# A fused attention and expert layer: other durations in the scheduler's table, and one more dependency for the weight conversions

## The chip, the cores and the metric

The program runs on one core of a Trainium2 chip. The metric is the device time of one execution in microseconds; for the kernel before it is 677.38 us, the median of three runs (677.03 to 679.04). The engines of the core have a queue each and work through it in order: TensorE (PE, with its weight loads as PEld), VectorE (DVE), ScalarE (ACT), GpSimd (POOL), and SyncE (SP), which here issues all transfers.

## The reference

The inputs are q, k, v of shape (4 batches, 12 heads, 448 positions, 64) and two weight matrices, 768 x 2048 and 2048 x 768, all float32.

```python
scores = scale * np.matmul(q, k.transpose(0, 1, 3, 2))
scores = np.where(mask, -1000000000.0, scores)          # causal
scores = scores - np.max(scores, axis=-1, keepdims=True)
attn = np.exp(scores)
attn = attn / (np.sum(attn, axis=-1, keepdims=True) + 1e-09)
x = np.matmul(attn, v)          # then (batch, head) x (seq, dim) -> 1792 tokens x 768
h = x @ w_in
g = h * np.clip(h + 3.0, 0.0, 6.0) / 6.0
out = g @ w_out
```

## The kernel before

Positions are cut into four tiles of C = 112. The first tile of all four batches (448 columns) is group 0; the remaining R = 336 positions of each batch are groups 1 to 4. For each group the attention of six head pairs gives x, and then the two dense layers run on it (`group`, L602): 16 chunks of w_in (768 columns each) make h, the gate gives g, and 24 chunks of w_out (512 columns) make the output.

For precision every operand of a dense layer is split into a rounded high part and the remainder: xh and xl, gh and gl, wh and wl, and for the scores op and kl. A product is three matmuls (`triple`, L596: L598, L599, L600), so a chunk of w_in takes 18 and a chunk of w_out 12. The high part is a cast by ScalarE or GpSimd (`move`: L238, L245), the remainder a subtraction by GpSimd or VectorE (`minus`: L250).

The weights come in as 64-bit words. In group 0 each chunk is turned into float32 bits on VectorE by three operations for each half chunk (L571, L573, L576; a w_out chunk has one such set), stored to `kept_w` for the later groups, cast and subtracted. The scratch of the conversion is a bank of tag "s".

The attention of group 0 (`first_pair`, L297) handles 112 rows of four batches at once: scores (L322, L329), row maxima (L336, L342), exponentials (L348, L360), sums (L363), `inverse` (L369, L370), normalisation on GpSimd (L377), transposes (L386), copies, and the product with v (L399). The attention of the others (`pair`, L410): scores (L453 in the first batch; L450 and L451 later), mask and row maximum in one VectorE operation (L476), exponential with its sum (L483), `inverse` (L492, L493), six normalisations per pair on GpSimd (L505, `scaled`), 18 transposes on PE in six turns (L516), copies, the product with v (L535). After the first dense layer of a chunk come ReLU (L621), the gate (L627), and the split into gh and gl. The accumulator has two banks ("mo"); L627 is the last to read one.

The order of the work is not written out by hand. A planner (`Flow`, L72) runs when the program is built: each operation has a key (its due time), its reads and writes, and the engines that can do it with a cost factor and a lag, as `{"P": 2, "D": (1, 1.0)}`: on GpSimd the base duration times 2, on VectorE times 1 but only from 1.0 us after it is ready. A free engine of the plan takes the ready operation with the lowest key whose buffers are free. What comes out is one fixed order for each engine; on the chip each engine follows its order and waits by semaphores. The base durations that matter here (n columns):

```python
def elem(n, psum=False):                 # minus, conversions
    return (n + 150) / 960
one(key, ways or {"A": 1}, (n + 200) / 1200, emit, r, w)     # move
```

Of the kernel before, what the change touches and what calls it, by code (L numbers as in the profile page):

```python
# [190 lines left out]
def tile_causal_attention_hardswish_moe(ctx: ExitStack, tc: tile.TileContext, q, k, v, w_in, w_out, out):  # L191
# [85 lines left out]
    def x_split(key, g, p, av, n):  # L277
        xh, xl = buf("xh", [128, S], F32R), buf("xl", [128, S], F32R)
        x_t[g, p] = xh, xl
        move(key, n, lambda: ap(xh)[:, :n], lambda: ap(av)[:, :n], [(av, 0)], [(xh, 0)], {"A": 1, "D": (1, .5)})  # L280
        y = av
        if g < 2:
            y = buf("r", [128, S])
            move(key, n, lambda: ap(y)[:, :n], lambda: ap(av)[:, :n], [(av, 0)], [(y, 0)], {"A": 1})
        minus(
            key + .01, n, lambda: ap(xl)[:, :n], lambda: ap(y)[:, :n], lambda: f(ap(xh)[:, :n]),
            [(y, 0), (xh, 0)], [(xl, 0)], {"P": 2, "D": (1, 1.0)} if g < 2 else {"D": 1},
        )
# [8 lines left out]
    def first_pair(p):  # L297
# [75 lines left out]
        one(t + 3.5, {"D": 1}, .5, inverse, [], sums)  # L373
# [36 lines left out]
    def pair(n):  # L410
# [15 lines left out]
        if b:  # L426
            for e in range(2):
                x, y, z = qk[e], op[e], kl[e]
                move(
                    t - 5, R + S, lambda x=x, y=y: ap(y), lambda x=x: ap(x), raw[4 * e:4 * e + 4] + [("step", t - 12)], [(y, 0), (y, 1)],  # L430
                    {"P": 1.1, "A": (1, .5)},
                )
                minus(
                    t - 4.9, S, lambda z=z: ap(z), lambda x=x: ap(x)[:, R:], lambda y=y: f(ap(y)[:, R:]),
                    [(x, 0, R), (x, 1, R), (y, 1)], [(z, 0)], {"D": 1, "P": (2, 1.0)},
                )
                minus(
                    t - 4.8, R, lambda y=y: ap(y)[64:, :R], lambda x=x: ap(x)[64:, :R], lambda y=y: f(ap(y)[64:, :R]),
                    [(x, 1, 0)], [(y, 0)], {"D": 1, "P": (2, 1.0)},
                )  # L440
# [57 lines left out]
        for e in range(2):  # L498
            for i in reversed(TILES):
                def scaled(g, e=e, i=i):  # L500
                    x, r = ap(pr[e, i]), ap(st)[:, e, 4 + i:5 + i]
                    if g == "A":
                        nc.scalar.activation(x, x, ACTF.Copy, scale=r)
# [3 lines left out]
                    t + 4.5 + .1 * e, {"P": 1}, (C * (i + 1) + 300) / 1100, scaled,  # L507
# [39 lines left out]
    def weights(g, i, t, early):  # L547
# [6 lines left out]
        else:  # L554
# [25 lines left out]
            for o in range(0, n, m):  # L580
# [6 lines left out]
                flow.op(t - T_W + .01, {"D": (1, 0)}, one_by_one, [(wd, 0)])  # L587
# [14 lines left out]
    def group(g):  # L602
# [3 lines left out]
        for i in range(NF):  # L606
# [19 lines left out]
            def gate(_, r=r, acc=acc):  # L626
# [9 lines left out]
                [(r, 0), (gh, i)], [(gl, i)], {"D": 1, "P": (1.9, .7)} if g else {"P": 2, "D": (1, 1.5)},  # L636
# [73 lines left out]
```

## Time and profile before

| | us |
|---|---|
| median of the runs | 677.38 |
| profiled execution | 677.73 |
| its span | 676.0 |
| busy PE / VectorE / ScalarE / GpSimd | 648.2 / 476.4 / 358.5 / 308.0 |

The span runs from the first to the last instruction. Busy time of an engine is the union of its instructions; for PE the ends of matmuls are modelled. A wait is put down to the engine that released it last. Durations of single instructions hold any time in which they were slowed, not only their bare work. Two numbers in a shape are partitions x elements. PEclk, the clock granted to PE, is given as a share of its upper level.

### The profile page before, as it was taken

To read this page: it belongs to the slowest core of one execution; us is meant where nothing else is said; L and a number is where in the kernel's file an instruction comes from. 1 tells how busy PE (TensorE), PEld (TensorE's weight loads), DVE (VectorE), ACT (ScalarE), POOL (GpSimd) and SP (SyncE) were. 2 spreads that over 40 slices of the span, in tenths; PEclk is the share of its full clock that TensorE was granted. 3 is DMA by queue.
4 is the path that set the end of the run, shared out by engine and by line. 5 is a ranking of instruction groups with operands and counts; after the bars stand their busy time and mean duration, and the time that the engine had idled before them with its cause. 6 is when DMAs were issued, how large, how long until landed. Compare 5 with 4: busy or idle time off the path is not lost.

```text
span 676.0 us, 12212 instructions
## 1 busy us (share of the span) xinstructions
PE 648.2 (96%) x4236; PEld 588.5 (87%) x4236; DVE 476.4 (70%) x945; ACT 358.5 (53%) x851; POOL 308.0 (46%) x346
## 2 busy tenths in 40 slices
PE   7789999999999989999999989999999999999998
PEld 5559878878788979999999879999889899999997
DVE  5999989986597877755688785666879743466432
ACT  3676565544446556555565555556545554444432
POOL 1558687655476266423356464442476502022000
PEclk9989999999999999999999999999999999999999
DMA  9998977796686544356844346556542334743452
GB/s 236 258 303 242 286 245 234 230 310 232 177 292 181 167 147 137 119 163 181 245 143 125 98 135 186 176 163 194 158 148 64 98 107 132 216 141 110 140 166 68
DMA packets 66877, 120.88 MB, mean 179 GB/s; under 512 B 16896, under 2 KB 33408, under 8 KB 66816
## 3 DMA queue, kind: packets, MB, share of 16 engines
q1 hardware_dynamic: 66816, 120.11, 59.1%
q8 instruction: 33, 0.54, 0.3%
q14 instruction: 28, 0.23, 0.1%
HBM read 101.99 MB, written 18.09 MB: 178 GB/s over the span
## 4 chain that ended last, share of the span: by engine, by line
PE 73%; POOL 10%; DVE 8%; issue 5%; ACT 2%; DMA 1%; SPq 1%; POOLq 0%; DVEq 0%; ACTq 0%
PE mo L598 19%; PE mo L600 18%; PE mo L599 18%; POOL pr L505 7%; PE s L535 6%; PE s L516 5%; PE s L450 2%; PE s L453 2%; PE s L451 2%; DVE wl L250 2%; DMA gh<-in_k_dram 1%; POOL gh L245 1%; SPq L229 1%; DVE r L627 1%; PE s L399 1%
## 5 line engine op out<-in xcount | busy, mean ns | idle before, releaser
L250 DVE TENSOR_TENSOR wl<-wd,wh 128x512 fp32r<-128x512 f32 (+1 forms) x155 | 141.3, 912 | 101.8 <-ACT wh L238 99.8
L238 ACT CAST wh<-wd 128x512 fp32r<-128x512 f32 (+1 forms) x160 | 112.8, 705 | 133.0 <-PE mo L599 100.4
L598 PE MATMUL mo<-xh,wh 128*128 128x336 f32 (+1 forms) x480 | 161.3, 336 | 2.7 <-DVE r L627 2.4
L598 PE MATMUL mo<-gh,wh 128*128 128x336 f32 (+1 forms) x480 | 160.3, 334 | 0.0
L600 PE MATMUL mo<-gh,wl 128*128 128x336 f32 (+1 forms) x480 | 156.5, 326 | 0.7 <-POOL wl L250 0.7
L599 PE MATMUL mo<-gl,wh 128*128 128x336 f32 (+1 forms) x480 | 156.5, 326 | 0.0
L600 PE MATMUL mo<-xh,wl 128*128 128x336 f32 (+1 forms) x480 | 156.3, 326 | 0.0
L599 PE MATMUL mo<-xl,wh 128*128 128x336 f32 (+1 forms) x480 | 155.5, 324 | 0.0
L505 POOL TENSOR_SCALAR pr<-pr,prow 112x224 f32<-112x224 f32 x144 | 105.5, 749 | 48.3 <-DVE prow L493 45.6
L598 PEld LDWEIGHTS mo<-xh,wh 128*128 128x128 f32 x480 | 90.5, 188 | 8.3 <-DVE r L627 5.2
L483 ACT ACTIVATE pr<-s,prow 112x448 f32<-112x448 f32 (+1 forms) x144 | 76.8, 540 | 36.4 <-DVE prow L476 36.3
L598 PEld LDWEIGHTS mo<-gh,wh 128*128 128x128 f32 x480 | 90.2, 188 | 4.2 <-issue 1.0
L600 PEld LDWEIGHTS mo<-gh,wl 128*128 128x128 f32 x480 | 90.2, 188 | 2.7 <-POOL wl L250 1.1
L599 PEld LDWEIGHTS mo<-xl,wh 128*128 128x128 f32 x480 | 91.0, 190 | 1.1
L599 PEld LDWEIGHTS mo<-gl,wh 128*128 128x128 f32 x480 | 90.3, 188 | 1.2
L600 PEld LDWEIGHTS mo<-xh,wl 128*128 128x128 f32 x480 | 90.2, 188 | 1.2
L476 DVE CUSTOM_DVE_ANT_0 s<-s,mask 112x448 f32<-112x448 f32 (+1 forms) x144 | 69.9, 532 | 25.0 <-PE s L451 19.9
L245 POOL TENSOR_SCALAR gh<-r 128x336 fp32r<-128x336 f32 x49 | 24.2, 494 | 116.4 <-DVE r L627 109.6
L250 POOL TENSOR_TENSOR wl<-op,wh 128x512 fp32r<-128x512 f32 (+1 forms) x38 | 56.9, 1498 | 37.6 <-ACT wh L238 35.3
L245 POOL TENSOR_SCALAR op<-qk 128x784 fp32r<-128x784 f32 x34 | 33.6, 993 | 74.9 <-PE s L451 64.0
L238 ACT COPY pt<-s 112x336 f32<-112x336 f32 x126 | 49.1, 443 | 25.9 <-PE s L516 25.6
L516 PE MATMUL s<-ident,pr 112*112 112x112 f32 x432 | 55.2, 261 | 7.0 <-POOL pr L505 6.6
(70 smaller groups left out, 868.6 us busy)
## 6 DMA issues: line engine op xcount, KB each, us to landing
wd<-kept_w SPq DMA_DIRECT2D x64, 384.0 KB, 3.8
wd<-kept_w SPq DMA_DIRECT2D x96, 256.0 KB, 2.7
wd<-in_w_in_dram SPq DMA_DIRECT2D x16, 768.0 KB, 6.3
wd<-in_w_out_dram SPq DMA_DIRECT2D x24, 512.0 KB, 5.2
qk<-in_k_dram SPq DMA_DIRECT2D x84, 112.0 KB, 2.9
qk<-in_q_dram SPq DMA_DIRECT2D x84, 84.0 KB, 2.8
kept_w<-op SPq DMA_DIRECT2D x16, 384.0 KB, 5.6
kept_w<-op SPq DMA_DIRECT2D x24, 256.0 KB, 5.6
```

What stands on the lines that cost most here:

```text
L238: nc.scalar.copy(o(), i()) if scale is None else nc.scalar.mul(o(), i(), scale)
L245: nc.gpsimd.tensor_scalar(o(), i(), 1.0, 1.0, ALU.mult, ALU.mult)
L250: (nc.gpsimd if e == "P" else nc.vector).tensor_tensor(o(), a(), b(), ALU.subtract)
L450: nc.tensor.matmul(dst, ap(op[e])[:, c], ap(op[e])[:, R:R + w], start=True, stop=False)
L476: lambda _, e=e, i=i, w=w, dst=dst: nc.vector.tensor_tensor_reduce(dst(), dst(), mask[:, S - w:], -0.125, 3.0e38, ALU.add, ALU.min, ap(st) ...
L483: lambda _, e=e, i=i, dst=dst: nc.scalar.activation(ap(pr[e, i]), dst(), ACTF.Exp, bias=ap(st)[:, e, i:i + 1], scale=-1.0, accum_out=ap(st ...
L505: nc.gpsimd.tensor_scalar(x, x, r, 1.0, ALU.mult, ALU.mult)
L516: nc.tensor.transpose(ap(tp)[:C, C * o:C * o + C], ap(pr[e, i])[:, C * j:C * j + C], ident)
L535: nc.tensor.matmul(ap(av)[64 * e:64 * e + 64, R - w:R], ap(vr)[:, j, e, :], ap(ph)[:, o:o + w], start=(j == 0), stop=(j == NC_ - 1),)
L598: nc.tensor.matmul(ps, ap(wh)[:, a], xh, start=start, stop=False)
L599: nc.tensor.matmul(ps, ap(wh)[:, a], xl, start=False, stop=False)
L600: nc.tensor.matmul(ps, ap(wl)[:, a], xh, start=False, stop=stop)
```

## The change

The cost factors of several subtractions and casts in the planner's table become larger, mostly those of GpSimd; the duration of a normalisation gets another formula. The reciprocal of each first pair (`inverse` in `first_pair`) also writes a token ("sums", p), and the conversion of every chunk but the first reads the token of the last pair, so that it is planned, and on the chip waits, behind that reciprocal. The rewritten call in `scaled` stands in a branch for ScalarE that no normalisation takes.

```diff
@@ -284,7 +284,7 @@
             move(key, n, lambda: ap(y)[:, :n], lambda: ap(av)[:, :n], [(av, 0)], [(y, 0)], {"A": 1})
         minus(
             key + .01, n, lambda: ap(xl)[:, :n], lambda: ap(y)[:, :n], lambda: f(ap(xh)[:, :n]),
-            [(y, 0), (xh, 0)], [(xl, 0)], {"P": 2, "D": (1, 1.0)} if g < 2 else {"D": 1},
+            [(y, 0), (xh, 0)], [(xl, 0)], {"P": 2.4, "D": (1, 1.0)} if g < 2 else {"D": 1},
         )
 
 
@@ -370,7 +370,7 @@
             nc.vector.reciprocal(r, r)
 
         sums = [(st, 0, 4)] + [(st, 1, 4 + b) for b in range(B)]
-        one(t + 3.5, {"D": 1}, .5, inverse, [], sums)
+        one(t + 3.5, {"D": 1}, .5, inverse, [], sums + [("sums", p)])
         for e in (1, 0):
             one(
                 t + 4, {"P": 1}, 1.05,
@@ -428,15 +428,15 @@
                 x, y, z = qk[e], op[e], kl[e]
                 move(
                     t - 5, R + S, lambda x=x, y=y: ap(y), lambda x=x: ap(x), raw[4 * e:4 * e + 4] + [("step", t - 12)], [(y, 0), (y, 1)],
-                    {"P": 1.1, "A": (1, .5)},
+                    {"P": 1.3, "A": (1, .5)},
                 )
                 minus(
                     t - 4.9, S, lambda z=z: ap(z), lambda x=x: ap(x)[:, R:], lambda y=y: f(ap(y)[:, R:]),
-                    [(x, 0, R), (x, 1, R), (y, 1)], [(z, 0)], {"D": 1, "P": (2, 1.0)},
+                    [(x, 0, R), (x, 1, R), (y, 1)], [(z, 0)], {"D": 1.25, "P": (2.2, 1.5)},
                 )
                 minus(
                     t - 4.8, R, lambda y=y: ap(y)[64:, :R], lambda x=x: ap(x)[64:, :R], lambda y=y: f(ap(y)[64:, :R]),
-                    [(x, 1, 0)], [(y, 0)], {"D": 1, "P": (2, 1.0)},
+                    [(x, 1, 0)], [(y, 0)], {"D": 1.3, "P": (2.6, 1.5)},
                 )
         st = buf("prow", [C, 2, 8])
         ps = {(e, i): bank("s") for i in TILES for e in range(2)}
@@ -500,11 +500,11 @@
                 def scaled(g, e=e, i=i):
                     x, r = ap(pr[e, i]), ap(st)[:, e, 4 + i:5 + i]
                     if g == "A":
-                        nc.scalar.activation(x, x, ACTF.Copy, scale=r)
+                        nc.scalar.mul(x, x, r)
                     else:
                         nc.gpsimd.tensor_scalar(x, x, r, 1.0, ALU.mult, ALU.mult)
                 one(
-                    t + 4.5 + .1 * e, {"P": 1}, (C * (i + 1) + 300) / 1100, scaled,
+                    t + 4.5 + .1 * e, {"P": 1}, min(.95, .2 + C * (i + 1) / 500), scaled,
                     [(st, e, 4 + i)], [(pr[e, i], 0)],
                 )
             for a, js in enumerate(((0,), (1,), (2, 3))):
@@ -584,7 +584,7 @@
                     (elem(m), lambda _, cv=cv, o=o, a=a: bits(cv, o, m, a), [[(cv, 0)], [(cv, 0)], [(wf, o)]][a])
                     for a in range(3)
                 ]
-                flow.op(t - T_W + .01, {"D": (1, 0)}, one_by_one, [(wd, 0)])
+                flow.op(t - T_W + .01, {"D": (1, 0)}, one_by_one, [(wd, 0)] + ([("sums", NPAIR - 1)] if i else []))
             dma(t - T_W, 512 * n, lambda: kept[i, :, :n], w, wk, [("kept", i)])
         move(t - T_W + .1, n, lambda: ap(wh)[:, :n], w, wk, [(wh, 0)], {"A": 1})
         minus(
@@ -633,7 +633,7 @@
             )
             minus(
                 t, n, lambda i=i: ap(gl)[:, i, :n], lambda r=r: ap(r)[:, :n], lambda i=i: f(ap(gh)[:, i, :n]),
-                [(r, 0), (gh, i)], [(gl, i)], {"D": 1, "P": (1.9, .7)} if g else {"P": 2, "D": (1, 1.5)},
+                [(r, 0), (gh, i)], [(gl, i)], {"D": 1.4, "P": (2.6, 1.0)} if g else {"P": 2.3, "D": (1.4, 1.5)},
             )
         for m in range(NK):
             acc, ob = bank("mo"), buf("r", [128, S])
```

## Rows read from the trace of the kernel before

**Rows 1.** The page, section 1: engine, busy us (share of the span) x instructions.

```profile
PE 648.2 (96%) x4236; PEld 588.5 (87%) x4236; DVE 476.4 (70%) x945; ACT 358.5 (53%) x851; POOL 308.0 (46%) x346
```

**Rows 2.** Windows: us, then busy of each engine (x instructions), clock, DMA share, GB/s.

```profile
24.00:49.00 25.00, 17.10 (x149) 11.07 (x145) 24.20 (x51) 18.20 (x56) 13.55 (x12) 0.86 0.91 270
49.00:160.00 111.00, 110.75 (x622) 93.81 (x622) 95.85 (x199) 62.27 (x144) 76.61 (x76) 1.00 0.83 267
160.00:212.00 52.00, 48.80 (x287) 41.60 (x284) 40.40 (x85) 25.67 (x66) 28.29 (x30) 1.00 0.69 209
212.00:560.00 348.00, 339.62 (x2317) 315.55 (x2317) 248.55 (x497) 196.24 (x471) 169.30 (x194) 1.00 0.50 148
```

**Rows 3.** Waits: engine, line <- awaited: us in total, times, longest.

```profile
PEld s L516 <- POOL pr L505: 10.0, 15, 1.5
...
PE s L516 <- POOL pr L505: 6.6, 12, 1.3
...
PEld mo L598 <- DVE r L627: 5.2, 9, 1.3
...
PE mo L598 <- DVE r L627: 2.4, 3, 1.1
```

**Rows 4.** Timeline of PE, 36 to 53 us: start, length, instruction [idle before].

```profile
45.64 0.99 PE L399 MATMUL s<-pt,gl 112*64 112x112 f32 x16 [0.73 <-ACT pt L238]
46.56 2.42 PE L453 MATMUL s<-qk 64*112 64x448 f32 x8
48.91 0.48 PE L598 MATMUL mo<-xh,wh 128*128 128x448 f32 x1
...
52.62 0.36 PE L598 MATMUL mo<-xh,wh 128*128 128x448 f32 x1
```

**Rows 5.** Timeline of VectorE, 35 to 42 us.

```profile
35.74 0.55 DVE L571 TENSOR_SCALAR s<-wd 128x384 int32<-128x384 int32 x1
...
40.71 0.61 DVE L363 TENSOR_REDUCE prow<-pr 112x4 f32<-112x448 f32 x1
...
41.56 0.20 DVE L370 RECIPROCAL prow<-prow 112x8 f32<-112x8 f32 x1
```

**Rows 6.** Timeline of ScalarE, 36 to 42 us.

```profile
38.02 0.58 ACT L360 ACTIVATE pr<-pr 112x448 f32<-112x448 f32 x1
```

**Rows 7.** Instructions of GpSimd by form: count, busy us, mean ns, idle before.

```profile
L505 POOL TENSOR_SCALAR pr<-pr,prow 112x448 f32<-112x448 f32 x48 | 41.1, 856 | 0.0
L505 POOL TENSOR_SCALAR pr<-pr,prow 112x336 f32<-112x336 f32 x48 | 39.3, 819 | 0.0
...
L505 POOL TENSOR_SCALAR pr<-pr,prow 112x224 f32<-112x224 f32 x48 | 27.4, 571 | 48.3 <-DVE prow L493 45.6 <-ACT wh L238 2.7
...
L250 POOL TENSOR_TENSOR gl<-r,gh 128x336 fp32r<-128x336 f32 x10 | 11.6, 1156 | 0.4
```

**Rows 8.** Timeline of PE around two pairs' transposes, 368 to 400 us.

```profile
370.27 0.88 PE L516 MATMUL s<-ident,pr 112*112 112x112 f32 x7 [0.74 <-POOL pr L505]
370.93 0.40 PE L598 MATMUL mo<-xh,wh 128*128 128x336 f32 x1
...
371.94 0.62 PE L516 MATMUL s<-ident,pr 112*112 112x112 f32 x2
372.86 0.88 PE L516 MATMUL s<-ident,pr 112*112 112x112 f32 x7 [0.30 <-POOL pr L505]
...
399.20 0.88 PE L516 MATMUL s<-ident,pr 112*112 112x112 f32 x7 [1.04 <-POOL pr L505]
```

**Rows 9.** Line L505: count, duration ns min/median/max, first and last start.

```profile
L505 POOL TENSOR_SCALAR pr<-pr,prow x144: 443/636/2430, 50.8 to 562.0; 112x224 f32<-112x224 f32 x48, 112x336 f32<-112x336 f32 x48, 112x448 f32<-112x448 f32 x48
```

**Rows 10.** Timeline of GpSimd, 388 to 400 us.

```profile
396.20 2.95 POOL L505 TENSOR_SCALAR pr<-pr,prow 112x336 f32<-112x336 f32 x2
```

**Rows 11.** Timeline of VectorE, 386 to 400 us.

```profile
396.25 1.03 DVE L250 TENSOR_TENSOR wl<-wd,wh 128x512 fp32r<-128x512 f32 x1
```

**Rows 12.** Instructions of VectorE by form, as rows 7.

```profile
L250 DVE TENSOR_TENSOR gl<-r,gh 128x336 fp32r<-128x336 f32 x54 | 41.3, 764 | 21.8 <-POOL gh L245 17.1 <-ACT gh L238 4.6
```

## The prediction

> **What bounds the kernel now.** I read the page's busy shares first: TensorE (PE) is busy 96% of the span, VectorE (DVE) 70%, GpSimd (POOL) 46% [rows 1]. So the matmuls set the time, and the change removes none of them: it can only win time in which PE waits. The second view is the busy time by stretch [rows 2]. PE is idle 7.9 us of the 25 us before the first group's mixture layer begins, 0.25 us of the next 111, 3.2 us from 160 to 212, and 8.4 us of the 348 us in which attention of one batch lies beside the matmuls of the one before. The third view is the list of waits [rows 3]: the largest single cause after the start is PE waiting for a GpSimd normalisation (L505) before a transpose (L516), 6.6 us in 12 waits on PE, 10.0 us as its weight loads saw it. Next comes the gate on VectorE (L627), which frees an accumulator bank: 2.4 and 5.2 us. All that this change can give is in those stretches.
>
> **The change, part by part.** The sum is made against the profiled execution, 677.73 us (span 676.0 and 1.7 around it), which stands 0.35 us above the median of 677.38.
>
> *The conversions that wait.* At the start VectorE's queue changes. Before, in front of the last first-group sum (L363, L369, L370; pr_475 is the probability tile of the sixth head pair, s a scratch bank of the conversion):
>
> ```order
> L356 TENSOR_TENSOR pr_475<-s,prow 112x448
> L571 TENSOR_SCALAR s<-wd 128x384
> L573 SCALAR_TENSOR_TENSOR s<-wd,s 128x384
> L576 SCALAR_TENSOR_TENSOR op<-wd,s 128x384
> L571 TENSOR_SCALAR s<-wd 128x384
> L573 SCALAR_TENSOR_TENSOR s<-wd,s 128x384
> L576 SCALAR_TENSOR_TENSOR op<-wd,s 128x384
> L571 TENSOR_SCALAR s<-wd 128x384
> L573 SCALAR_TENSOR_TENSOR s<-wd,s 128x384
> L576 SCALAR_TENSOR_TENSOR op<-wd,s 128x384
> L363 TENSOR_REDUCE prow<-pr_475 112x4
> L369 TENSOR_SCALAR prow<-prow 112x2x4
> ```
>
> The same place now (pr_468 is the same tile, numbered anew):
>
> ```order
> L356 TENSOR_TENSOR pr_468<-s,prow 112x448
> L476 ISA s,prow<-s,mask 112x448
> L476 ISA prow 112x1
> L363 TENSOR_REDUCE prow<-pr_468 112x4
> L369 TENSOR_SCALAR prow<-prow 112x2x4
> L370 RECIPROCAL prow<-prow 112x2x4
> L571 TENSOR_SCALAR s<-wd 128x384
> L573 SCALAR_TENSOR_TENSOR s<-wd,s 128x384
> L576 SCALAR_TENSOR_TENSOR op<-wd,s 128x384
> ```
>
> Nine conversion operations move behind the reciprocal, and one masking operation comes in front of it; three more conversion operations move out from in front of the fifth pair's sums. On PE's queue the rows in front of the first expert matmul (L598) were:
>
> ```order
> L399 MATMUL s<-pt_595,gl 64x112
> L399 MATMUL s<-pt_593,gl 64x112
> L453 MATMUL s<-qk 112x448 x2
> L453 MATMUL s<-qk 112x336 x2
> L598 MATMUL mo<-xh,wh 128x448
> ```
>
> and are now:
>
> ```order
> L453 MATMUL s<-qk 112x224 x2
> L386 MATMUL mo<-ident,pr_468 112x112 x4
> L399 MATMUL s<-pt_577,gl 64x112
> L399 MATMUL s<-pt_544,gl 64x112
> L598 MATMUL mo<-xh,wh 128x448
> ```
>
> The four score matmuls (L453) of a later pair go behind the first chunks: the same work later, so their 2.35 us (46.56 to 48.91) are moved and not won [rows 4]. What is won is the earlier end of the sums. The nine operations stand from 35.74 to 40.71, 4.97 us [rows 5]. The masking operation in their place I put at the 0.6 us of the sum beside it, so the last reciprocal can end 4.4 us earlier; with the three others (a third of 4.97, 1.7) 6.0. At the least it is 2.1 us: ScalarE's exponential that L363 sums ended at 38.60 even in its old place [rows 6], and ScalarE's queue now has it in front of two copies. From the end of the last reciprocal (41.76) to the end of the last first-group product (46.63) it was 4.9 us [rows 4, 5], which stays. PE's clock was 0.86 of its upper level in that stretch [rows 2], so PE ran part of it at the lower of its two levels, after idling; a second such stretch would cost 0.14 x 25 = 3.5 us. Bounds for the start: from 6.0 us won to 2.1 - 3.5 = 1.4 lost. I take 4.3, by the row of the nine operations.
>
> The wait added: the twelve conversion operations (6.6 us) now stand in front of the first masked scores and gates of VectorE. What hides them: VectorE idles 15.2 of the 111 us from 49 to 160 [rows 2]. The nearest need is chunk 1: PE wants it 4.9 us plus one chunk (48.91 to 52.62, 3.7 us) after the last reciprocal [rows 4], 8.6 us; its conversion takes 3.3 us and leaves 5.3 for the cast and the subtraction behind it. SyncE's queue has the stores of converted chunks and the loads behind them in nearly the same order, and a load is issued about four chunks ahead. If that cover were gone, the most that comes back is the 6.6 us.
>
> *The costs in the planner.* They change no operation, only the planner's belief. It held a normalisation of 224, 336 and 448 columns to take 0.48, 0.58 and 0.68 us; measured are 0.571, 0.819 and 0.856 [rows 7]; now it holds 0.65, 0.87 and 0.95. What follows is seen on PE's queue in the 15th pair (head 0's last transpose of pr_4453, then head 1's first of pr_4544). Before:
>
> ```order
> L516 MATMUL s<-ident,pr_4453 112x112 x2
> L598 MATMUL mo<-xh,wh 128x336
> L599 MATMUL mo<-xl,wh 128x336
> L600 MATMUL mo<-xh,wl 128x336
> L598 MATMUL mo<-xh,wh 128x336
> L599 MATMUL mo<-xl,wh 128x336
> L600 MATMUL mo<-xh,wl 128x336
> L516 MATMUL s<-ident,pr_4544 112x112
> ```
>
> Now (pr_4435 and pr_4534 are those tiles):
>
> ```order
> L516 MATMUL s<-ident,pr_4435 112x112 x2
> L598 MATMUL mo<-xh,wh 128x336
> L599 MATMUL mo<-xl,wh 128x336
> L600 MATMUL mo<-xh,wl 128x336
> ...
> L598 MATMUL mo<-xh,wh 128x336
> L599 MATMUL mo<-xl,wh 128x336
> L600 MATMUL mo<-xh,wl 128x336
> L516 MATMUL s<-ident,pr_4534 112x112
> ```
>
> Twelve matmuls stand between the heads where six did; six take 1.0 us (370.93 to 371.94) [rows 8]. Counted through the whole order, from a pair's last score matmul to its first transpose there are six matmuls more (0.9 us) and to head 1's twelve more (1.8 us) in most pairs of groups 1 to 4. The waits there are 0.74 and 0.30 us (370.27, 372.86) [rows 8], the longest of all 1.3 [rows 3]: head 1's are covered, head 0's 0.74 too. In the 16th and 22nd pair, which wait 1.04 us each (399.20), the distance shrinks by 1.3 us, but GpSimd's queue there has lost two subtractions from between the normalisations:
>
> ```order
> L505 TENSOR_SCALAR pr_4811<-pr_4811,prow 112x224
> L505 TENSOR_SCALAR pr_4766<-pr_4766,prow 112x336
> L250 TENSOR_TENSOR gl<-r,gh 128x336
> L245 TENSOR_SCALAR gh<-r 128x336
> L505 TENSOR_SCALAR pr_4727<-pr_4727,prow 112x448
> L505 TENSOR_SCALAR pr_4815<-pr_4815,prow 112x224
> L250 TENSOR_TENSOR gl<-r,gh 128x336
> L505 TENSOR_SCALAR pr_4777<-pr_4777,prow 112x336
> ```
>
> became
>
> ```order
> L505 TENSOR_SCALAR pr_4763<-pr_4763,prow 112x224
> L505 TENSOR_SCALAR pr_4745<-pr_4745,prow 112x336
> L505 TENSOR_SCALAR pr_4730<-pr_4730,prow 112x448
> L245 TENSOR_SCALAR gh<-r 128x336
> L505 TENSOR_SCALAR pr_4791<-pr_4791,prow 112x224
> L505 TENSOR_SCALAR pr_4753<-pr_4753,prow 112x336
> ```
>
> Two gl subtractions are 2 x 1.156 = 2.3 us [rows 7], more than the 1.3 lost. So I take all 6.6 us of PE's waits as gone; bounds are 10.0 (the weight loads' count) and a loss of 2.6 (1.3 in each of those two pairs).
>
> Here a row speaks against the premise. A normalisation's length is no constant: 443 ns at the least, 2430 at the most [rows 9]. The pair of them begun at 396.20 took 2.95 us [rows 10] while VectorE's subtraction of 396.25 ran 1.03 us and others followed [rows 11]. The Trainium skill (SBUF — State Buffer, "SBUF: two separate sides") says that VectorE operations with two SBUF inputs and GpSimd operations that read SBUF take one port pair by turns, each holding it to its end. The rows agree. By that rule the new costs are a mean of waits, and part of the late normalisations outlast any fixed distance; by a fixed length all 6.6 us go. That is a rival below.
>
> *Work that changes engine.* Over the whole order VectorE gets 10 gl, 4 kl and 7 wl subtractions more, and gives up 10 of op to GpSimd and 18 casts and copies to ScalarE; VectorE's total moves by under 3 us of 476. It is at 70% and hidden, but its gate L627 stands behind these subtractions. I put it at nothing; bounds are the 2.4 us that its waits cost now, and the rival below. The stretch 160 to 212 I leave as it is: one conversion moved in front of masked sums that wait for PE, others stay behind theirs; bounds plus and minus its 3.2 us.
>
> Sum: 677.73 - 4.3 - 6.6 = 666.8 us.
>
> **The rivals.**
> - *The normalisations still come late* because their length varies. For it: the spread [rows 9]. Against it: the distances grew by more than most waits. Half of 6.6 stays: 670.1 us.
> - *The start is not won*: conversions now late, or PE at its lower clock again. For it: VectorE is busy 24.2 of 25 us there. Against it: the 15.2 us of later idle. 677.73 - 6.6 = 671.1 us.
> - *The change does not do what it says*: both fail, waits only move. 677 us.
> - *Slower: the gate.* In groups 1 to 4 each of 64 gates L627 frees one of two accumulator banks, and ten more gl subtractions (0.764 us each [rows 12]) and seven of wl stand in front of some. A wait of a weight load for it is now 5.2 / 9 = 0.58 us [rows 3]. If 32 gates are late by that, 18.6 - 5.2 = 13.4 us come in: 677.73 - 10.9 + 13.4 = 680.2 us. It decides from 28 late gates, (10.9 + 5.2) / 0.58. Against it: nine wait now, and the planner's price of those subtractions on VectorE rises too (0.51 to 0.71 us for gl, measured 0.764).
>
> **How the numbers follow.** The forecast has 0.46 and by itself 663 to 669.5. Late normalisations 0.17, start not won 0.13, neither won 0.13, the gate 0.11. A measurement of this kernel can tell about 0.3% (2 us) from no change. Faster: 0.46 + 0.17 + 0.13 = 0.76; same 0.13; slower 0.11. The range runs from 662, where both upper bounds (6.0 and 10.0) are won, to 676, which leaves out the gate and a part of no change.
>
> **What would show it.** Right: the last first-group reciprocal ends near 37.4 instead of 41.76; the first L598 starts near 42.3 instead of 48.91 and PE does not wait for conversions behind it; PE's waits for L505 fall from 6.6 to under 1.5 us; those for L627 stay near 2.4. Wrong: PE idle reappears from 45 to 100 us (conversions late), the waits for L505 stay above 3 us, or L627 heads the list.

## The result, and the profile after

The changed kernel takes 661.53 us (median of 4 runs, 661.49 to 661.94) against 677.2 us (677.01 to 679.04) for the kernel before beside it: a ratio of 0.9764, 95% interval 0.9747 to 0.9782. It is faster, as forecast, but by 15.7 us and not by 10.9: 0.5 us under the range. The first section of its page answers [rows 1]:

```profile
PE 643.9 (98%) x4236; PEld 587.3 (89%) x4236; DVE 465.8 (71%) x939; ACT 367.3 (56%) x870; POOL 301.2 (46%) x333
```

The windows, with the columns of [rows 2]:

```profile
24.00:49.00 25.00, 18.32 (x150) 13.51 (x149) 21.61 (x48) 17.41 (x53) 15.90 (x13) 0.80 0.87 251
49.00:160.00 111.00, 110.45 (x617) 92.90 (x616) 98.62 (x205) 63.44 (x148) 72.16 (x73) 1.00 0.83 262
160.00:212.00 52.00, 51.75 (x304) 43.60 (x303) 39.20 (x84) 27.10 (x69) 26.02 (x29) 1.00 0.79 245
212.00:560.00 348.00, 348.00 (x2420) 327.13 (x2419) 245.52 (x497) 209.93 (x502) 171.41 (x191) 1.00 0.51 152
```

From 212 to 560 us PE is never idle, where it idled 8.4 us, and from 160 to 212 it idles 0.25 where it idled 3.2 [rows 2]. Nearly all the idle time that is left before 560 us lies at the start (6.7 of the 25 us from 24 to 49), and there the clock is lower, 0.80 for 0.86. The waits of PE's queue, longest first, then those of its weight loads for the gate:

```profile
PE s L329 <- DMA gh<-in_k_dram: 2.9, 3, 2.1
PE mo L386 <- POOL pr L377: 2.7, 2, 2.4
PE s L322 <- DVE maskr L273: 2.3, 1, 2.3
PE s L399 <- ACT pr L483: 1.8, 1, 1.8
PE s L399 <- DVE pt L241: 1.4, 1, 1.4
...
PEld mo L598 <- DVE r L627: 1.2, 4, 0.5
```

The two groups that headed [rows 3] are gone from PE: every wait of 0.5 us or more that is left is at the start. Where the 16.2 us of span went is read from the start times of the 960 first matmuls of a product (L598; the same number of them, in the same order of chunks, in both kernels; they are counted from 0):

| from the k-th L598 to the next | before, us | after, us | difference |
|---|---|---|---|
| span's start to 48th | 82.34 | 82.25 | -0.1 |
| 48th to 96th | 41.56 | 42.03 | +0.5 |
| 96th to 192nd | 83.87 | 81.03 | -2.8 |
| 192nd to 384th | 126.33 | 120.57 | -5.8 |
| 384th to 768th | 250.21 | 241.64 | -8.6 |
| 768th to 959th | 87.88 | 88.48 | +0.6 |

The attention matmuls between them do not fall into the same stretches in both kernels. A block of 16 products with v (L535) takes 1.85 us of PE in either. The changed kernel does one block fewer than the kernel before from the 192nd to the 384th (80 matmuls for 96) and one more from the 384th to the 768th (192 for 176); and eight score matmuls (1.2 us) moved from the 96th to the 192nd into the stretch behind. So on equal work it wins about 1.6 us from the 96th to the 192nd, 5.1 to the 384th and 10.4 to the 768th.

From the 192nd to the 768th (14.3 us won, with equal products), the intervals between PE's instructions, sorted by what stands at their two ends, say where: from transpose to transpose 35.7 before and 26.4 after (-9.3), from a score matmul to an expert matmul 7.6 and 4.4 (-3.2), all others together -1.8. The wins are a few long intervals: before, 15 from transpose to transpose were over 0.1 us longer than the usual 0.096, by 9.4 us together, and three from score to expert matmul were longer than the usual 0.153, by 3.0 us together; after, one of the first kind is left, by 0.1, and none of the second.

**How a wait went.** The 15th pair of the prediction is seen best on GpSimd and PE. Before, GpSimd and then PE (start, length; the wait of 370.27 stands behind the second transpose [rows 8]):

```profile
365.80 1.45 POOL L250 TENSOR_TENSOR gl<-r,gh 128x336 fp32r<-128x336 f32 x1
367.23 1.93 POOL L505 TENSOR_SCALAR pr<-pr,prow 112x224 f32<-112x224 f32 x2
```

```profile
359.81 0.27 PE L451 MATMUL s<-kl,op 128*112 128x224 f32 x1
369.12 0.41 PE L516 MATMUL s<-ident,pr 112*112 112x112 f32 x2
```

After:

```profile
356.89 3.33 POOL L250 TENSOR_TENSOR kl<-qk,op 128x448 fp32r<-128x448 f32 x2
360.64 4.22 POOL L505 TENSOR_SCALAR pr<-pr,prow 112x224 f32<-112x224 f32 x4 [0.43 <-DVE prow L493]
```

```profile
352.94 0.27 PE L451 MATMUL s<-kl,op 128*112 128x224 f32 x1
364.30 1.03 PE L516 MATMUL s<-ident,pr 112*112 112x112 f32 x9
```

From the last score matmul to the first transpose PE had 9.3 us of other work before (359.81 to 369.12) and has 11.4 now (352.94 to 364.30). The normalisations themselves are no faster: these four took 1.05 us each, where the two before took 0.97. On GpSimd a gl subtraction of 1.45 us stood in front of them, and the first started 1.25 us behind the end of its reciprocal (365.98); now it starts 0.17 us behind it (360.47). The nine transposes run in one piece. Over all 144 the normalisations got longer, not shorter: the sums of the three forms are 111.4 us, 773 ns each, and were 107.8 us, 749 ns [rows 7]. They still spread [rows 9]:

```profile
L505 POOL TENSOR_SCALAR pr<-pr,prow x144: 445/645/1737, 54.8 to 544.6; 112x224 f32<-112x224 f32 x48, 112x336 f32<-112x336 f32 x48, 112x448 f32<-112x448 f32 x48
```

So their length still varies (the longest is 1737 ns for 2430), and the distance outlasts it. The Trainium skill's rule that VectorE's operations with two SBUF inputs and GpSimd's that read SBUF take one port pair by turns (SBUF — State Buffer, "SBUF: two separate sides") agrees with that spread: beside VectorE's subtractions of two SBUF tiles a normalisation of 224 columns took 0.757 us, beside its other work 0.457 (last section). A rival that followed from such a spread, late normalisations in spite of the distance, did not come.

**The start.** The reciprocal came as early as forecast (VectorE):

```profile
36.04 0.61 DVE L363 TENSOR_REDUCE prow<-pr 112x4 f32<-112x448 f32 x1
...
36.89 0.20 DVE L370 RECIPROCAL prow<-prow 112x8 f32<-112x8 f32 x1
```

It ends at 37.09 instead of 41.76 [rows 5], 4.67 us earlier. PE did not follow:

```profile
36.51 1.76 PE L399 MATMUL s<-pt,gl 112*64 112x112 f32 x16
...
41.89 0.59 PE L386 MATMUL mo<-ident,pr 112*112 112x112 f32 x4
44.28 0.99 PE L399 MATMUL s<-pt,gl 112*64 112x112 f32 x16 [1.80 <-ACT pr L483]
45.20 0.48 PE L598 MATMUL mo<-xh,wh 128*128 128x448 f32 x1
...
46.27 0.58 PE L599 MATMUL mo<-xl,wh 128*128 128x448 f32 x1
46.64 0.58 PE L600 MATMUL mo<-xh,wl 128*128 128x448 f32 x1
...
50.11 0.36 PE L599 MATMUL mo<-xl,wh 128*128 128x448 f32 x1
50.31 0.36 PE L600 MATMUL mo<-xh,wl 128*128 128x448 f32 x1
```

and GpSimd, between the reciprocal and the last normalisation of the first pairs (L377):

```profile
37.26 0.93 POOL L377 TENSOR_TENSOR pr<-pr,prow 112x448 f32<-112x448 f32 x1 [2.00 <-DVE prow L370]
39.36 1.14 POOL L250 TENSOR_TENSOR xl<-r,xh 128x448 fp32r<-128x448 f32 x1 [1.16 <-ACT r L238]
40.45 0.94 POOL L377 TENSOR_TENSOR pr<-pr,prow 112x448 f32<-112x448 f32 x1
```

The plan put a subtraction (xl) between the last two normalisations; it waits for a copy on ScalarE, which waits for the product L399 of 36.51, which runs at the low clock (1.76 us; the same 16 matmuls of 40.40 take 0.99). The last L377 therefore starts 2.3 us after it could have. The first L598 starts at 45.20 instead of 48.91, 3.71 us earlier. Of these, 2.35 us are the score matmuls (L453) that now come later [rows 4]. Then the granted clock falls a second time; the window 46 to 49 us, with the columns of [rows 2], shows PE busy throughout at half of the upper level, 1.2 GHz:

```profile
46.00:49.00 3.00, 3.00 (x10) 2.69 (x9) 2.90 (x7) 1.54 (x4) 2.65 (x2) 0.50 1.05 382
```

The matmuls of 46.27 and 46.64 start 0.37 us apart, those of 50.11 and 50.31 0.20 apart. Nine of them, from 45.91 to 49.25, take 3.34 us, and would take 1.80 at the later spacing: 1.54 lost. 3.71 - 2.35 - 1.54 = -0.18: all of it is spent. By the 48th L598 PE has done the same matmuls in both kernels, and it is there at 82.25 instead of 82.34: nothing is won.

### The profile page after: what moved, and what is told of

It reads as the page before. It is cut to its first block, busy times and chain, and to the rows that moved or that the text cites. A ratio compares the mean times of both kernels' runs of the same rounds, so it can differ in the third digit from the quotient of the medians.

```text
span 659.8 us, 12245 instructions
## 1 busy us (share of the span) xinstructions
PE 643.9 (98%) x4236; PEld 587.3 (89%) x4236; DVE 465.8 (71%) x939; ACT 367.3 (56%) x870; POOL 301.2 (46%) x333
## 4 chain that ended last, share of the span: by engine, by line
PE 92%; DVE 3%; DMA 1%; SPq 1%; ACT 1%; POOL 1%; issue 1%; DVEq 0%; ACTq 0%; POOLq 0%
PE mo L598 24%; PE mo L600 23%; PE mo L599 23%; PE s L535 6%; PE s L516 6%; PE s L450 3%; PE s L451 2%; PE s L453 2%; DMA gh<-in_k_dram 1%; SPq L229 1%; PE s L399 1%; DVE s L571 1%; DVE s L573 1%; DVE op L576 0%; PE s L329 0%
## 5 line engine op out<-in xcount | busy, mean ns | idle before, releaser
L250 DVE TENSOR_TENSOR wl<-wd,wh 128x512 fp32r<-128x512 f32 (+1 forms) x159 | 142.8, 898 | 99.8 <-ACT wh L238 99.5
L598 PE MATMUL mo<-xh,wh 128*128 128x336 f32 (+1 forms) x480 | 160.8, 335 | 0.1
L598 PE MATMUL mo<-gh,wh 128*128 128x336 f32 (+1 forms) x480 | 159.2, 332 | 0.0
L505 POOL TENSOR_SCALAR pr<-pr,prow 112x224 f32<-112x224 f32 x144 | 109.0, 773 | 39.5 <-DVE prow L493 39.3
L245 POOL TENSOR_SCALAR gh<-r 128x336 fp32r<-128x336 f32 x51 | 33.3, 654 | 138.2 <-DVE r L627 128.6
L598 PEld LDWEIGHTS mo<-xh,wh 128*128 128x128 f32 x480 | 91.0, 190 | 5.8 <-issue 1.7
L598 PEld LDWEIGHTS mo<-gh,wh 128*128 128x128 f32 x480 | 90.3, 188 | 2.8 <-issue 0.8
L483 ACT ACTIVATE pr<-s,prow 112x448 f32<-112x448 f32 (+1 forms) x144 | 76.9, 542 | 25.7 <-DVE prow L476 25.7
L250 POOL TENSOR_TENSOR wl<-op,wh 128x512 fp32r<-128x512 f32 (+1 forms) x35 | 53.3, 1522 | 44.1 <-ACT wh L238 34.3
L238 ACT COPY pt<-s 112x336 f32<-112x336 f32 x139 | 53.3, 446 | 26.0 <-PE s L516 25.9
L621 ACT ACTIVATE r<-mo,three 128x336 f32<-128x336 f32 (+1 forms) x80 | 44.7, 558 | 26.4 <-PE mo L600 20.9
L245 POOL TENSOR_SCALAR op<-qk 128x784 fp32r<-128x784 f32 x31 | 30.4, 985 | 57.3 <-PE s L451 54.0
```

Of the source, the lines that this page charges most:

```text
L238: nc.scalar.copy(o(), i()) if scale is None else nc.scalar.mul(o(), i(), scale)
L245: nc.gpsimd.tensor_scalar(o(), i(), 1.0, 1.0, ALU.mult, ALU.mult)
L250: (nc.gpsimd if e == "P" else nc.vector).tensor_tensor(o(), a(), b(), ALU.subtract)
L483: lambda _, e=e, i=i, dst=dst: nc.scalar.activation(ap(pr[e, i]), dst(), ACTF.Exp, bias=ap(st)[:, e, i:i + 1], scale=-1.0, accum_out=ap(st ...
L505: nc.gpsimd.tensor_scalar(x, x, r, 1.0, ALU.mult, ALU.mult)
L598: nc.tensor.matmul(ps, ap(wh)[:, a], xh, start=start, stop=False)
```

## The experiments

Each ratio is against the kernel before on the same chip in the same rounds. "Groups 3 and 4" is the stretch from the 384th to the 768th L598, where the order repeats pair by pair; "T-T" is the time from transpose to transpose in it; "passage" is the 144th to the 288th L598, from group 0 to group 1; "48th" is its start. In the stretch "groups 3 and 4" nearly all the attention of these two (11 of 12 pairs) runs beside the dense layers of groups 2 and 3. The number in brackets counts the products with v (L535) in the stretch: where it is 16 lower, 1.9 us of work lie elsewhere, and have to be added before two rows are compared. The kernel with the costs twice as far also has 9 transposes (0.9 us) fewer in the passage and 9 more in groups 3 and 4. The stretches come from one profiled execution of each kernel; those of the changed kernel and of the one with filler agree within 0.1 us.

| kernel | ratio [95%] | 48th | passage (L535) | groups 3 and 4 (L535) | T-T |
|---|---|---|---|---|---|
| before | 1 | 82.34 | 107.6 (80) | 250.2 (176) | 24.2 |
| changed | 0.9764 [0.9747, 0.9782] | 82.25 | 100.8 (80) | 241.6 (192) | 17.2 |
| dependency alone | 1.0005 [0.9989, 1.0021] | 83.78 | 107.7 (80) | 250.2 (176) | 24.1 |
| all costs, no dependency | 0.9818 [0.9787, 0.9849] | 81.52 | 104.3 (64) | 241.7 (192) | 17.2 |
| normalisation's cost alone | 0.9954 [0.9928, 0.998] | 82.12 | 105.9 (64) | 249.0 (192) | 22.0 |
| all costs but that | 0.9884 [0.9856, 0.9913] | 81.33 | 106.4 (80) | 243.1 (176) | 20.7 |
| costs half as far | 0.9885 [0.9859, 0.9912] | 84.13 | 102.5 (64) | 245.0 (176) | 21.9 |
| costs twice as far | 0.9796 [0.9765, 0.9826] | 84.53 | 97.7 (64) | 242.5 (192) | 17.6 |
| costs of op and kl alone | 0.9904 [0.9873, 0.9936] | 81.75 | 103.9 (64) | 245.2 (176) | 21.2 |
| changed, token of fifth pair | 0.9821 [0.9786, 0.9856] | 83.09 | 105.3 (80) | 241.7 (192) | 17.2 |
| changed, filler | 0.9797 [0.9753, 0.9841] | 84.48 | 100.8 (80) | 241.6 (192) | 17.2 |
| changed, L377 earlier | 0.9821 [0.9795, 0.9848] | 83.82 | 103.0 (64) | 242.3 (192) | 17.2 |
| changed, xl's cost back | 0.9849 [0.9814, 0.9884] | 82.68 | 103.0 (64) | 241.7 (192) | 17.2 |

On 192 products, groups 3 and 4 of the kernel before are 252.1: the changed kernel wins 10.4 us there, the normalisation's cost alone 3.1, all costs but that 7.2, op and kl alone 5.0, the half step 5.2 and the double step 10.4.

**The dependency alone.**

```diff
-        one(t + 3.5, {"D": 1}, .5, inverse, [], sums)
+        one(t + 3.5, {"D": 1}, .5, inverse, [], sums + [("sums", p)])
...
+                flow.op(t - T_W + .01, {"D": (1, 0)}, one_by_one, [(wd, 0)] + ([("sums", NPAIR - 1)] if i else []))
```

> The kernel before with the added dependency alone (conversions of chunks 1 to 39 wait for the sixth pair's reciprocal), old costs. Theory A (the start wins nothing, because the copies, the low clock and the queue of PE come out later by as much): 676 to 678 us, waits of PE for L505 still about 6.6 us. Rival B (the start is won as forecast and something else in the changed kernel hid it): about 673 us. Rival C (the dependency costs, the costs repay it): 679 us or more.

The time does not change: 1.0005. The first L598 starts at 44.34, 4.6 us earlier, and the 48th at 83.78, 1.4 later. PE's waits for L505 stay those of before, and one for the gate is added:

```profile
PE s L516 <- POOL pr L505: 6.8, 13, 1.3
...
PE mo L598 <- DVE r L627: 3.8, 4, 1.8
```

The new wait stands at the start, for a gate behind a conversion on VectorE, and soon after it the granted clock is at the lower level while PE is busy (timeline of PE; window):

```profile
54.14 0.47 PE L598 MATMUL mo<-xh,wh 128*128 128x448 f32 x1 [1.83 <-DVE r L627]
```

```profile
55.00:58.40 3.40, 3.40 (x11) 3.04 (x10) 3.24 (x7) 1.52 (x3) 2.58 (x2) 0.51 0.70 156
```

**All costs, without the dependency.** The two lines above left as they were.

> The kernel before with all new costs and without the added dependency. Theory A: 660 to 663 us, the whole change. Rival B: about 666 us, the start missing. Rival C: below 660 us.

0.9818 (666.35 us): the whole gain of groups 3 and 4 without the dependency, and my figure for it missed, since some 5 us of the changed kernel are not here. They lie in the passage: on 80 products it takes 106.2, 5.4 more than in the changed kernel. The number is rival B's, but its reason, a start that is missing, is not what happened: the 48th L598 comes at 81.52, earlier than in the changed kernel.

**The normalisation's cost alone.**

```diff
-                    t + 4.5 + .1 * e, {"P": 1}, (C * (i + 1) + 300) / 1100, scaled,
+                    t + 4.5 + .1 * e, {"P": 1}, min(.95, .2 + C * (i + 1) / 500), scaled,
```

> The kernel before with the new duration of a normalisation alone. Theory A (the waits for L505 were worth some 9 us counted by the distance from one transpose to the next, the rest of the gain comes with the other costs through the gate L627): 667 to 669 us, waits for L505 under 2 us, those for L627 about as before. Rival D (this entry makes it all): 661 to 663 us. Rival E (a reordering by luck, not the entry): over 672 us with waits for L505 above 4 us.

675.01 us: this missed by far. I had taken the new formula for what moves the transposes; alone it takes a third of their waits away. Time and waits are those that rival E (luck of the order) named; the half and the double step below speak against E in groups 3 and 4. PE's waits:

```profile
PE s L516 <- POOL pr L505: 4.4, 9, 0.8
...
PE mo L598 <- DVE r L627: 0.6, 2, 0.4
```

**All costs but the normalisation's.** The line above left as it was, the five others changed.

> The kernel before with the new costs of subtractions and casts alone, the duration of a normalisation as before, no dependency. Theory A: 670 to 673 us, the waits for L627 gone, those for L505 at some 3 to 6 us. Rival D: 676 to 678 us. Rival E: anything, with both kinds of waits still there.

670.8 us, as expected, but the waits for the gate are still there. More of the gain comes with the costs of what stands in front of the normalisations on GpSimd than with their own:

```profile
PE s L516 <- POOL pr L505: 3.1, 6, 0.7
PE mo L598 <- DVE r L627: 2.2, 2, 1.1
```

In groups 3 and 4, T-T falls by 2.2 with the one part, 3.5 with the other and 7.0 with both. This fits a late normalisation being the sum of what the plan under-counts on GpSimd in front of it, so that what one part leaves uncounted is still late; no run shows that sum itself. A rival, that the gain comes from work that left GpSimd's queue, can be set against the traces: over the twelve pairs of groups 3 and 4 the last normalisation of a pair ends 11.05 us behind the pair's last score matmul in the kernel before and 10.92 in the changed one, while the first transpose starts 8.7 and 9.6 us behind it (9.1 with either part alone). The transposes came later, the normalisations hardly earlier.

**Half and double the step.** Each cost moved half as far as in the change, and twice as far, without the dependency; for op:

```diff
-                    {"P": 1.1, "A": (1, .5)},
+                    {"P": 1.2, "A": (1, .5)},
```

```diff
-                    {"P": 1.1, "A": (1, .5)},
+                    {"P": 1.5, "A": (1, .5)},
```

> All the changed costs halfway between old and new, no dependency. Theory F (a wait for a normalisation is the sum of what the plan under-counts on GpSimd since the queues last agreed, so it shrinks with the error): groups 3 and 4 (from the 384th to the 768th L598) take some 245 to 247 us, between the 250.2 of before and the 241.7 of the new costs; the whole 669 to 673 us, waits for L505 2 to 4 us. Rival L (luck of the order): 250 us or under 242 for the two groups.

> All the changed costs moved twice as far as the change moved them, no dependency. Theory F: waits for L505 at nothing, and groups 3 and 4 take 241 to 242.5 us as with the new costs, since no wait is left to remove; the whole 663 to 668 us by what the first groups do. Rival G (a turn that is planned too late costs as much as one too early, through banks and buffers held longer): groups 3 and 4 over 245 us. Rival L: over 248 us with waits for L505.

T-T falls with the step, 24.2, 21.9 and 17.2 us at none, half and the whole, and no further at double (17.6): once the distance covers the wait, more of it buys nothing. On equal work the half step gives 5.2 of the 10.4 us of groups 3 and 4, and the double step the same 10.4 as the whole. With the double step no wait of PE for L505 is left in the list, and with the half one 2.8 us.

**The costs of op and kl alone.**

```diff
-                    {"P": 1.1, "A": (1, .5)},
+                    {"P": 1.3, "A": (1, .5)},
...
-                    [(x, 1, 0)], [(y, 0)], {"D": 1, "P": (2, 1.0)},
+                    [(x, 1, 0)], [(y, 0)], {"D": 1.3, "P": (2.6, 1.5)},
```

> Only the new costs of the cast and the two subtractions of q and k (op and kl), all else as before. Theory F: these stand in front of the normalisations in GpSimd's queue, so most of the 6.9 us that the new costs of subtractions and casts gave: 671 to 673 us, groups 3 and 4 in 244 to 247 us. Rival H (the gl and first-group costs made it, through the gate L627): 675 to 678 us, 249 to 250 us.

671.38 us, T-T 21.2: most of what all costs but the normalisation's give, 3.0 of 3.5 in T-T and 5.0 of 7.2 us in groups 3 and 4. The rest there is left to gl; xl's cost works on groups 0 and 1 alone.

**The token of the fifth pair.** The changed kernel, whose conversions wait for the fifth pair's sums instead of the sixth's.

```diff
+                flow.op(t - T_W + .01, {"D": (1, 0)}, one_by_one, [(wd, 0)] + ([("sums", NPAIR - 2)] if i else []))
```

> The changed kernel, its dependency taken from the fifth pair's reciprocal instead of the sixth's. Theory T (the dependency's 4.8 us on top of the new costs are the luck of another order at the passage from group 0 to group 1, 190 to 250 us): anything from 661 to 667 us, with the same groups 3 and 4 (241.7 us) and the difference in the stretch from the 144th to the 288th L598. Rival B (the dependency itself removes something): 661 to 662.5 us, as the changed kernel, since the conversions still wait for nearly all sums.

Groups 3 and 4 keep their 241.7, and the passage loses 4.6 us (105.3 for 100.8), nearly as much as the changed kernel had over the kernel with the costs alone. The gain in the passage does not go with the dependency as such: with the double costs and without any dependency the passage is as short (97.7, on equal work 100.4).

**Filler for the clock.** 24 matmuls of 64 columns at three places from the fifth pair on, into bank columns that nothing reads.

```diff
+            if p > 3:
+                for _ in range(24):
+                    nc.tensor.matmul(ap(ps[1])[:C, S:512], identr, maskr[:, 0, :64], start=True, stop=True)
...
+                if p == NPAIR - 1 and e == 0:
+                    for _ in range(24):
+                        nc.tensor.matmul(ap(tp)[:C, S:512], identr, maskr[:, 0, :64], start=True, stop=True)
```

> The changed kernel with filler: 24 extra matmuls of 64 columns into unused columns of a bank, behind the score products of first pairs 5 and 6 and behind the first head of the sixth pair's last product, whose results nothing reads. Theory C (what the earlier reciprocals of the first pairs won at the start was lost to the second stretch at the low granted clock, 45.9 to 49.3 us, about 1.7 us): with TensorE kept busy there the second stretch goes, the 48th L598 comes at 80.0 to 81.0 instead of 82.25, time 658.5 to 660.5 against 661.5 for the changed kernel. Rival (the work around the first L598 is bound by the conversions and copies, the clock costs nothing in the end): the 48th L598 at 82 or later, time 661.5 to 664 with the filler's own time on top.

The second stretch at the low clock did not go; it came later, behind the later first L598 (47.87). The windows of this kernel, columns as in [rows 2]:

```profile
46.00:49.50 3.50, 2.55 (x20) 2.25 (x21) 3.37 (x8) 2.94 (x8) 0.79 (x2) 0.77 1.02 415
49.50:53.00 3.50, 3.50 (x15) 3.18 (x14) 3.33 (x10) 1.69 (x7) 2.47 (x2) 0.74 1.05 333
```

From the 24th L598 on everything is 2.2 us later than in the changed kernel and otherwise the same. The third block of filler runs 2.3 us past the transposes in front of it (to 45.70), and ScalarE's copy behind them waits for it; PE is idle for 1.25 us behind the filler. This run therefore does not test what the clock costs.

**The first pairs' normalisations earlier.**

```diff
-                t + 4, {"P": 1}, 1.05,
+                t - 8, {"P": 1}, 1.05,
```

> The changed kernel with the first pairs' normalisations (L377) keyed 12 earlier in the plan, so that on GpSimd they stand ahead of the subtraction xl that stood before the last of them. Theory Q (the distance from the last reciprocal of the first pairs to the first L598, 8.1 us after and 7.2 before, holds some 3 us in which the last L377 waits behind xl): the distance falls to 5 to 6 us, the first L598 near 42.5 to 43.5, the 48th 2 to 3 us earlier than 82.25, if the passage from group 0 to 1 keeps its order time 658.5 to 660. Rival (the clock and the conversions take it back): first L598 earlier, 48th within 0.5 us of 82.25, time 661 to 662. In either case a changed order after 120 us can move the total by up to 5 us (Theory T); the 48th L598 is what decides.

The distance from the last reciprocal to the first L598 falls from 8.1 to 4.2 us, but the reciprocal itself now ends at 40.40, the first L598 starts at 44.63, and the 48th is 1.6 us later, not 2 to 3 earlier. Theory Q has the distance right and the gain wrong. As with the dependency alone, PE then waits 1.83 us for a gate (before 54.37), and from 55.9 to 59.2 us the granted clock is 0.50 with PE busy.

**The one cost of xl back.**

```diff
-            [(y, 0), (xh, 0)], [(xl, 0)], {"P": 2.4, "D": (1, 1.0)} if g < 2 else {"D": 1},
+            [(y, 0), (xh, 0)], [(xl, 0)], {"P": 2, "D": (1, 1.0)} if g < 2 else {"D": 1},
```

> The changed kernel with the one cost of the subtraction xl on GpSimd set back from 2.4 to 2: the normalisations, casts and other subtractions keep the new costs, the dependency stays. Theory F (what groups 3 and 4 win is bought by the distances that come from the costs of normalisation, kl, op, cast and gl): the 384th to the 768th L598 takes 241.6 again (241.0 to 242.5). Theory T (the passage from group 0 to group 1 is luck of the order): the 144th to the 288th takes anything from 98 to 106 us, total 659 to 667. Rival (the cost of xl is what makes the passage good): the 144th to the 288th at 104 or more, total 665 or more; if it stays at 100.8 and 661.5, that cost does nothing.

Groups 3 and 4 keep 241.7 and T-T 17.2, which the costs of the others were to buy. The passage takes 103.0, on 80 products 104.9, 4.1 us more than in the changed kernel, from one number that only works on groups 0 and 1 (the 2.0 us more of the 96th to the 144th L598 are a block of products that lies there). So the rival, that this cost makes the passage good, is not ruled out. This run also bears on the clock at the start. There is no second stretch at the low clock in it; PE (timeline) waits instead:

```profile
52.58 0.37 PE L600 MATMUL mo<-xh,wl 128*128 128x448 f32 x1
54.81 0.47 PE L598 MATMUL mo<-xh,wh 128*128 128x448 f32 x1 [1.86 <-DVE r L627]
```

for a gate that stands on VectorE behind a conversion:

```profile
52.38 0.60 DVE L571 TENSOR_SCALAR s<-wd 128x384 int32<-128x384 int32 x1
53.02 0.56 DVE L573 SCALAR_TENSOR_TENSOR s<-wd,s 128x384 int32<-128x384 int32 x1
53.67 0.56 DVE L576 SCALAR_TENSOR_TENSOR op<-wd,s 128x384 int32<-128x384 int32 x1
54.14 0.61 DVE L627 SCALAR_TENSOR_TENSOR r<-r,mo 128x448 f32<-128x448 f32 x1
```

Behind this wait the clock stays at the upper level:

```profile
55.00:58.00 3.00, 3.00 (x16) 2.81 (x16) 2.90 (x6) 2.20 (x4) 1.86 (x3) 1.00 0.94 266
```

The kernels with the dependency alone and with L377 earlier wait 1.83 us at the same place, the one with the costs alone and the one with all costs but the normalisation's 1.1. The 48th L598 of this one starts at 82.68.

## Why the prediction was wrong, point by point

- **The bound and the direction: right.** The gain is PE's idle time, and 212 to 560 us is where most of it was.
- **The range, 662 to 676: its lower end was too high.** It added the upper bounds of the start and of the waits, 6.0 and 10.0, and left out those of the two terms put at nothing, 2.4 for the gate and 3.2 for 160 to 212 us. These two came, and the start did not.
- **The reciprocal, 37.4 forecast: right** (37.09).
- **The start, -4.3: wrong; -0.1 measured at the 48th L598, +0.4 at the 96th.** The step that failed is the 4.9 us from the end of the last reciprocal to the end of the last first-group product, "which stays": in the changed kernel it is 8.2, and the first L598 starts at 45.20 and not near 42.3. An earlier reciprocal helps only so far. Where it ends at 40.16, 40.40 and 40.83 us (the dependency alone, L377 earlier, xl's cost back) the first L598 starts 4.2 us behind it, at 44.34, 44.63 and 45.01; where it ends at 37.09 and 38.24 (the changed kernel, the costs alone), 8.1 and 6.6 us behind it, at 45.20 and 44.88. In these two a product L399 on the way waits for an exponential of a later pair (L483), 1.80 us before 44.28 and 0.70 before 41.25. The rival "start not won" named the right outcome. Its two reasons both turned up: the low clock from 46 to 49 us in the changed kernel (1.5 us, where 3.5 were put), a gate behind the conversions in five others (two of them without the dependency), and in two of these, the dependency alone and L377 earlier, the low clock behind the gate as well. The 48th L598 comes at 83.8 in the two that have both, and at 81.3 to 82.7 in the four that have one. No run shows which one thing holds the first L598 at 44 to 45, nor what would be won if neither came.
- **The waits for L505, -6.6: right in kind, too small; -9.3 measured** from the 192nd to the 768th L598. The failed step is the choice of the row: PE's own idle time (6.6) over the count of its weight loads (10.0) [rows 3], which I kept as a bound only. The idle time runs from the modelled end of a matmul to the next start, and PE loses more than that: the transpose of 399.20, with 1.04 us of idle time [rows 8], started 1.2 us late by the usual distance of two transposes. The 15 long intervals are as many as the waits of the weight loads. That all of these waits go, though the normalisations' length varies, held. The forecast put this on the normalisation's formula and on the subtractions; the runs show that each alone leaves nearly half or more of the waits.
- **Work that changes engine, 0 for the gate L627: wrong by about 3 us.** Its waits of 2.4 us fell out of PE's list, and the intervals from a score matmul to an expert matmul lost 3.2 us. I had looked only for a loss there. In groups 3 and 4 this part (2.1 us) comes with the normalisation's cost alone, with the others alone and with op and kl alone alike, so it is not tied to one entry of the table, and not to gl's price on VectorE; why the gates are no longer late stays open. VectorE's busy time fell by 10.6 us [rows 1], where a move of under 3 was forecast.
- **160 to 212 us, 0 with bounds of 3.2: the bound was reached** (2.95 us of idle time gone). The passage as a whole gave 6.8 us, from the 144th to the 288th L598, on the same number of products. PE's idle time in it was 5.0 us before, 1.8 of it for L505 and 1.1 for the gate, and is 0.25. On equal work the passage takes 100.4 to 107.8 us over the kernels and follows neither the size of the step (107.6, 104.4, 106.2 and 100.4 at none, half, the whole and double) nor the dependency (107.7 with it alone). Of the 6.8 us, 1.4 come with the costs alone, and three small changes to the changed kernel lost 4.1 to 4.6 of them. I take the rest for luck in how the order fell; that is an inference, and no run shows what sets the order there. This is why 661.5 and not 666 us was measured: the kernel with the costs alone, 666.35, stands within half a microsecond of the forecast, though by other terms, and that is luck too.
- **The sum by what was measured:** 677.73 - 9.3 - 3.2 - 1.8 (192nd to 768th) - 2.8 (96th to 192nd) + 0.4 (start) + 0.6 (end) = 661.6 us.
- **The slower rival, the gate: did not come.** None of the kernels was measurably slower than before.

## What to carry to other kernels

In a plan for in-order queues, the error that mattered here is, as far as the runs tell, the sum of all that is under-counted on a queue in front of the awaited instruction; correcting the awaited instruction alone gave 2.7 of some 16 us. Once the planned distance covered the wait here, costs that were too high had no price in the stretch that repeats (twice the step: 10.4 us won there, as with the whole), so counting too much was safer than counting too little. And a small change of a planner's table is a new draw for every stretch that does not repeat: here such a stretch moved by up to 7 us between tables, so a gain should be sought in the stretches that do repeat, and the rest be treated as chance until a run shows its cause. Before a stretch is compared between two orders, count what each does in it: here one block of products across its border was worth 1.9 us.

## What the runs showed of the hardware

- In the changed kernel the clock fell to its lower level a second time, 0.7 us after the first expert matmul, though PE was busy then; PE had been idle for 1.80 us before 44.28. With the dependency alone and with L377 earlier it fell behind an idle time of 1.83 us. In the kernel with xl's cost back PE was idle 1.86 us before 54.81 and the clock stayed at the upper level behind it. Idle times of nearly one length were followed by a fall in three kernels and by none in the fourth.
- A normalisation slows beside some of VectorE's work, and VectorE beside GpSimd. In the changed kernel, 40 of the normalisations of 224 columns ran for over half of their length beside VectorE's work and took 0.755 us, and four ran alone at 0.452. The slow ones are those that met subtractions of two tiles in SBUF (L250): 26 that met only these took 0.757 us, and 10 that met only other work of VectorE 0.457. With 336 columns it is 0.869 (16) and 0.548 (11), with 448 0.843 (25) and 0.644 (12), alone 0.547 and 0.643. On VectorE, 34 subtractions of wl (128x512) beside GpSimd took 0.951 us, 51 alone 0.692. The form of 224 columns, the first of each head, got slower by the change:

```profile
L505 POOL TENSOR_SCALAR pr<-pr,prow 112x448 f32<-112x448 f32 x48 | 40.1, 834 | 0.0
L505 POOL TENSOR_SCALAR pr<-pr,prow 112x336 f32<-112x336 f32 x48 | 36.8, 766 | 0.0
L505 POOL TENSOR_SCALAR pr<-pr,prow 112x224 f32<-112x224 f32 x48 | 34.5, 719 | 39.5 <-DVE prow L493 39.3
```

  It was 571 ns [rows 7] and is 719. All the same no transpose on PE's list waits for it.
